# One input tile loaded in two column parts over two queues, and one late weight loaded whole

## The chip, the cores and the metric

The kernel runs on one core of one Trainium2 chip. The metric is device time in microseconds (us) of one execution. Inputs and outputs lie in HBM; all arrays are bfloat16.

## The reference

A block of a two-stream diffusion transformer: image tokens (2 x 256) and text tokens (2 x 32), width D = 1152. A condition vector `c` makes shift, scale and gate vectors for each stream.

```python
mod_i = (silu(c) @ wmod_img).reshape(B, 6, 1, D)
shi, sci, gai = mod_i[:, 0], mod_i[:, 1], mod_i[:, 2]
hi = layernorm(x_img) * (1 + sci) + shi
qi, ki, vi = split(hi @ wqkv_img, 3)
...
q = concat([qt, qi]); k = concat([kt, ki]); v = concat([vt, vi])
p = softmax(einsum('bqd,bkd->bqk', q, k) * D ** -0.5)
at, ai = split(einsum('bqk,bkd->bqd', p, v))
out_i = x_img + gai * (ai @ wo_img)
out_t = x_txt + gat * (at @ wo_txt)
```

The text stream is treated as the image stream, with its own weights. Only the first three of the six parts of `wmod_img` and `wmod_txt` are used.

## The kernel before

**Tiles.** The 512 image rows are four tiles of 128 rows (`x_i[:, i, :]`, i = 0 to 3, 288 KB each; tiles 0 and 1 are batch 0). D is cut into 9 blocks of 128 (`KT`) for contraction and into 3 chunks of 384 (`CH`) for statistics. Weights are [128, 9, 1152] tiles of 2592 KB; most of them rotate through a pool of five buffers (`wpool`, `load_w`, L73 to L77). Some 39 MB of weights go through in one execution.

**Order.** The schedule is written out by hand (`manual_schedule`, L62): each engine works through its instructions in program order, and a DMA is issued by the queue of the engine named in its call: `nc.sync` is SyncE (SP in the profile), `nc.scalar` is ScalarE (ACT). Waits between engines come from the tiles that the instructions read and write.

**The front, L80 to L116.** SyncE issues `c` (L81). Tiles 0 and 1 of x go on ScalarE's queue (L100). Then SyncE issues in this order: scale chunk 0 (`load_sc(0)`, blocks 0 and 1 of the image scale weight, 576 KB), x tile 2, two rows of the V weight (`load_v(0)`, 288 KB each), scale chunk 1, two V rows, scale chunk 2, two V rows, scale chunk 3 (864 KB), a V row, x tile 3, two V rows in one, and then the image shift weight and the image Q weight in three parts each. All later weights are issued by SyncE too (L433 to L443), each as soon as its buffer is free.

**The first work.** TensorE runs 15 warm-up matmuls on zeros (L286, L288) around the transpose of `c`. VectorE takes the layernorm statistics of tile 0, three instructions of 384 columns (`ln_stats`, L166), combines them (L171), does the same for tile 1, and then normalises tile 0 and tile 1 (L179). ScalarE takes the roots (L173). TensorE's program order is: the 18 matmuls of scale chunk 0 (`mod_scale(0)`, L218), the transposes of tile 0 (L197, L209), those of tile 1, and then V of the image tiles (`v_row`, L256; `v_narrow`, L268) between the matmuls of the further scale chunks. ScalarE scales the first two blocks while it moves them out of PSUM (`head_scaled`, L202).

**The V phase and after.** V is accumulated block by block as the V rows and scale chunks arrive, up to 28.5 us. The image shift follows (`mod_strip`, L404), then Q and K of the image (`qk_img`, L504), from 60 us on the text stream's shift and scale, then scores, softmax, attention output and the output projections.

**The text scale weight.** `w_sc_t` (L435) is loaded in two parts (`K2`: blocks 0 to 4, 1440 KB, and blocks 5 to 8, 1152 KB), after the text shift weight `w_sh_t` and ahead of the text tokens `x_t` (L436). It is read by the second `mod_strip` in `row_strips` (L522).

Of the kernel before, what the change touches and what calls it, by code (L numbers as in the profile page):

```python
# [14 lines left out]
def kernel(  # L15
# [14 lines left out]
    nc = tc.nc  # L30
# [4 lines left out]
    B, NI, D = x_img.shape  # L35
# [5 lines left out]
    TPB = NI // P  # L41
    NTT = B * NT
    CH = 384
# [24 lines left out]
    xi_t = xi_flat.rearrange("(i p) d -> p i d", p=P)  # L68

    def w_view(src):  # L70
        return src.rearrange("(kt p) n -> p kt n", p=P)

    def load_w(src, c0, ksplits=((0, KT),), home=None):  # L73
        t = wpool.tile([P, KT, D], bf, tag="w", name="t") if home is None else act.tile([P, KT, D], bf, tag=home, name="w_home")
        for (k0, k1) in ksplits:
            nc.sync.dma_start(t[:, k0:k1, :], w_view(src)[:, k0:k1, c0:c0 + D])
        return t  # L77
# [4 lines left out]
    x_i = act.tile([P, NIT, D], bf)  # L82
# [6 lines left out]
    def load_x(i, eng=nc.sync):  # L89
        eng.dma_start(x_i[:, i, :], xi_t[:, i, :])  # L90

    def load_sc(ch):
        k0, k1 = KC[ch]
        nc.sync.dma_start(w_sc_i[:, :, k0 * P:k1 * P], w_view(wmod_img)[:, :, D + k0 * P:D + k1 * P])
# [2 lines left out]
        for kt in range(*KC[ch]):  # L97
            nc.sync.dma_start(w_v_i[:, kt:kt + 1, :], w_view(wqkv_img)[:, kt:kt + 1, 2 * D:3 * D])

    for i in range(TPB):  # L100
        load_x(i, nc.scalar)
    load_sc(0)
    load_x(2)
    load_v(0)
# [9 lines left out]
    K2 = ((0, 5), (5, KT))  # L114
# [317 lines left out]

    w_k_i = load_w(wqkv_img, D, K3)  # L433
    w_sh_t = load_w(wmod_txt, 0)
    w_sc_t = load_w(wmod_txt, D, K2)  # L435
    nc.sync.dma_start(x_t[0:P:P // NTT, :], xt_flat[:, :])  # L436
    w_q_t = load_w(wqkv_txt, 0, K2)
    w_k_t = load_w(wqkv_txt, D, K2)
# [465 lines left out]
```

## Time and profile before

| | |
|---|---|
| three runs | 114.66, 114.88, 114.92 us; median 114.88 |
| the profiled execution | 114.55 us, span 112.7 us |
| TensorE matmul (PE) busy | 107.6 us, 95% of the span |
| TensorE weight load (PEld) busy | 64.1 us, 57% |
| VectorE (DVE) busy | 76.2 us, 68% |
| ScalarE (ACT) busy | 36.5 us, 32% |
| GpSimd (POOL) busy | 28.1 us, 25% |
| DMA | 40.87 MB, mean 363 GB/s over the span |
| SyncE's queue (q1) | 39.05 MB, 90.4% of the 16 DMA engines' span |
| granted TensorE clock | 1.0 throughout |

The span is the time from the first to the last instruction of the profiled execution; its own time is a little longer than that. PE and PEld are two rows for one engine, as weight loads overlap matmuls. A DMA of 128 rows is spread over 16 DMA engines, and it has landed when the last of them has reported. The chain of waits goes back from the last instruction to what released it, step by step.

### The profile page before, as it was taken

How to read it: one execution, taken by the hardware profiler on the slowest of the kernel's cores; microseconds unless marked ns; L12 is line 12 of the kernel's file. 1: busy time of each engine (PE TensorE's matmuls, PEld its weight loads, DVE VectorE, ACT ScalarE, POOL GpSimd, SP SyncE). 2: the span in 40 equal slices, each digit the busy share in tenths (PEclk: the TensorE clock that was granted, in tenths of full speed). 3: DMA queues.
4: the chain of work that ended last, by engine and by line, in shares of the span. 5: the costliest groups of instructions: out<-in, count | busy, mean ns of one | idle time of the engine just before them, and what ended most of it. 6: DMA issues, size and time to landing. Idle time of an engine off the chain costs nothing.

```text
span 112.7 us, 2837 instructions
## 1 busy us (share of the span) xinstructions
PE 107.6 (95%) x1182; PEld 64.1 (57%) x1191; DVE 76.2 (68%) x151; ACT 36.5 (32%) x83; POOL 28.1 (25%) x62
## 2 busy tenths in 40 slices
PE   5989999999999999999999999999999999999990
PEld 1356665565544444444446558787687565667670
DVE  1699330865499999999999950238657700899971
ACT  4527500471280080730009933024647700001000
POOL 7000120830230000000000161601540460499600
PEclk9999999999999999999999999999999999999999
DMA  3999999999999999999999999999999999994052
GB/s 90 321 376 347 373 373 407 409 413 411 405 410 408 411 410 413 404 412 410 413 410 414 413 403 408 404 398 404 410 407 401 411 422 394 383 371 168 7 192 70
DMA packets 22839, 40.87 MB, mean 363 GB/s; under 512 B 1375, under 2 KB 6635, under 8 KB 22827
## 3 DMA queue, kind: packets, MB, share of 16 engines
q1 hardware_dynamic: 21547, 39.05, 90.4%
q10 hardware_dynamic: 672, 0.77, 2.2%
q0 software_dynamic: 608, 0.88, 2.2%
q8 instruction: 9, 0.15, 0.5%
q14 instruction: 3, 0.02, 0.1%
HBM read 39.36 MB, written 1.34 MB: 361 GB/s over the span
## 4 chain that ended last, share of the span: by engine, by line
PE 89%; DVE 4%; DMA 3%; ACT 1%; issue 1%; ACTq 0%
PE qkps L504 31%; PE ps L826 16%; PE va L256 14%; PE aps L734 5%; PE ps L565 4%; PE sps L594 4%; PE gps L404 3%; DMA x_i<-in_x_img_dram 3%; DVE stats L166 3%; PE ops L844 2%; PE van L268 2%; PE ps L669 2%; PE mps L218 1%; ACT hT_i L202 1%; PE gps L799 1%; PE sps L607 1%
## 5 line engine op out<-in xcount | busy, mean ns | idle before, releaser
L504 PE MATMUL qkps<-hT_i,t 128*128 128x512 bf16 x158 | 35.4, 379 | 0.2
L504 PEld LDWEIGHTS <-t 128*128 128x128 bf16 x162 | 15.6, 98 | 18.7 <-DMA t<-in_wqkv_img_dram 0.3
L466 DVE SCALAR_TENSOR_TENSOR sacc<-w_v_i,mcols,sacc 128x1152 f32<-128x1152 bf16 x16 | 22.7, 1418 | 0.5
L256 PE MATMUL va<-w_v_i,hT_i 128*128 128x512 bf16 x67 | 17.0, 379 | 0.4 <-issue 0.2
L826 PE MATMUL ps<-t,aT 128*128 128x384 bf16 x99 | 16.4, 326 | 0.0
L826 PEld LDWEIGHTS <-aT 128*128 128x128 bf16 x117 | 11.0, 98 | 6.9 <-issue 0.5
L832 DVE TENSOR_TENSOR tmp<-ps,gb 128x384 bf16<-128x384 f32 x11 | 6.0, 548 | 6.5 <-DMA gb<-mod_scratch 6.0
L810 POOL TENSOR_TENSOR w_og<-t,gb 128x384 bf16<-128x384 bf16 x9 | 8.7, 1007 | 5.2 <-DMA gb<-mod_scratch 5.2
L256 PEld LDWEIGHTS <-hT_i 128*128 128x128 bf16 x72 | 6.4, 97 | 5.8 <-issue 0.2
L523 POOL TENSOR_SCALAR mod_txt<-mcols 128x18 f32<-128x18 f32 x2 | 0.6, 275 | 32.4 <-DVE mcols L410 32.4
L166 DVE BATCH_NORM_STATS2 stats<-x_i 128x6 f32<-128x384 bf16 x12 | 5.8, 541 | 2.6 <-DMA x_i<-in_x_img_dram 2.6
L454 ACT ACTIVATE qT<-qkps 128x512 bf16<-128x512 f32 x9 | 4.7, 601 | 6.9 <-PE qkps L504 6.9
L140 PE MATMUL wps<-wz 128*128 128x512 bf16 x15 | 5.6, 536 | 1.2 <-DVE wz L125 1.2
L470 ACT CAST shi<-sacc 128x1152 bf16<-128x1152 f32 x2 | 2.3, 1152 | 13.2 <-DVE sacc L466 13.2
L241 POOL TENSOR_SCALAR hT_i<-hT_i,mod_img 128x128 bf16<-128x128 bf16 (+1 forms) x5 | 2.1, 437 | 14.9 <-ACT hT_i L202 8.5
L747 DVE TENSOR_SCALAR aT<-aps,sv 128x288 bf16<-128x288 f32 (+2 forms) x11 | 4.3, 455 | 2.0 <-PE aps L734 2.0
L833 DVE TENSOR_TENSOR o<-tmp,x_i 128x384 bf16<-128x384 bf16 x11 | 5.3, 479 | 0.4
L565 PEld LDWEIGHTS <-t 128*128 128x128 bf16 x162 | 5.0, 98 | 0.5
L154 DVE CAST kT<-qkps 128x512 bf16<-128x512 f32 x3 | 2.1, 686 | 4.7 <-PE qkps L504 4.7
L565 PE MATMUL ps<-hT_t,t 128*128 128x64 bf16 x162 | 5.0, 193 | 0.0
L734 PE MATMUL aps<-pT,v_i 128*128 128x288 bf16 (+2 forms) x44 | 4.8, 264 | 0.0
L749 ACT ACTIVATE aT<-aps,sv 128x288 bf16<-128x288 f32 (+2 forms) x11 | 4.0, 468 | 2.1 <-PE aps L734 2.1
(150 smaller groups left out, 141.6 us busy)
## 6 DMA issues: line engine op xcount, KB each, us to landing
t<-in_wqkv_img_dram SPq DMA_DIRECT2D x6, 864.0 KB, 13.7
t<-in_wmod_txt_dram SPq DMA_DIRECT2D x2, 2592.0 KB, 18.2
t<-in_wqkv_txt_dram SPq DMA_DIRECT2D x2, 1440.0 KB, 14.3
t<-in_wmod_img_dram SPq DMA_DIRECT2D x3, 864.0 KB, 11.7
t<-in_wqkv_txt_dram SPq DMA_DIRECT2D x3, 864.0 KB, 14.0
t<-in_wo_txt_dram SPq DMA_DIRECT2D x3, 864.0 KB, 15.3
t<-in_wqkv_txt_dram SPq DMA_DIRECT2D x2, 1152.0 KB, 15.0
w_v_i<-in_wqkv_img_dram SPq DMA_DIRECT2D x7, 288.0 KB, 6.7
```

Source lines behind the costliest of these rows:

```text
L140: nc.tensor.matmul(ps[:], lhsT=wz[:, 0:P], rhs=wz[:], start=True, stop=True)
L166: nc.vector.bn_stats(stats[0:np_, k, :], x_ap[:, k * CH:(k + 1) * CH])
L256: nc.tensor.matmul(ps[:], lhsT=hT_i[:, kt, i * P:(i + 1) * P], rhs=w_v_i[:, kt, half * VW:(half + 1) * VW], start=(kt == 0), stop=(kt == K ...
L454: nc.scalar.mul(out_ap, in_ap, SCALE)
L466: nc.vector.scalar_tensor_tensor(saccs[b][:], w_v_i[:, kt, :], ap, saccs[b][:], op0=ALU.mult, op1=ALU.add)
L504: nc.tensor.matmul(pss[j - j0][:], lhsT=wq[:, kt, j * P:(j + 1) * P], rhs=hT_i[:, kt, :], start=(kt == 0), stop=(kt == KT - 1))
L565: nc.tensor.matmul(ps[:, j - j0, :], lhsT=wq[:, kt, j * P:(j + 1) * P], rhs=hT_t[:, kt, :], start=(kt == 0), stop=(kt == KT - 1))
L734: nc.tensor.matmul(bank[:, off:off + c1 - c0], lhsT=lhsT, rhs=rhs, start=(first[id(bank)] == n), stop=(final[id(bank)] == n))
L810: nc.gpsimd.tensor_mul(w_og[:, dt, 0:CH], w_o_i[:, dt, NG0:D], gb[:, B - 1, NG0:D])
L826: nc.tensor.matmul(ps[:, 0:cw], lhsT=aT[:, dt, t0:t0 + P], rhs=rhs, start=(dt == DTS[0]), stop=(dt == DTS[-1]))
L832: nc.vector.tensor_mul(tmp[:, 0:cw], ps[:, 0:cw], gb[:, b, cs])
L833: nc.vector.tensor_add(o[:, cs], tmp[:, 0:cw], x_i[:, i, cs])
```

## The change

Two places change. Tile 0 of x, one transfer of 128 x 1152 on ScalarE's queue, becomes two: columns 0 to 383 stay first on ScalarE's queue, and columns 384 to 1151 go on SyncE's queue, after `c` and ahead of scale chunk 0. Tile 1 stays on ScalarE's queue, behind the first part. The text scale weight `w_sc_t`, two transfers on SyncE's queue, becomes one of 2592 KB. The number of DMAs in the program stays the same. No arithmetic changes.

```diff
@@ -97,8 +97,9 @@
-    for i in range(TPB):
-        load_x(i, nc.scalar)
+    nc.scalar.dma_start(x_i[:, 0, 0:CH], xi_t[:, 0, 0:CH])
+    nc.sync.dma_start(x_i[:, 0, CH:D], xi_t[:, 0, CH:D])
+    load_x(1, nc.scalar)
     load_sc(0)
     load_x(2)
     load_v(0)
@@ -432,7 +433,7 @@
     w_k_i = load_w(wqkv_img, D, K3)
     w_sh_t = load_w(wmod_txt, 0)
-    w_sc_t = load_w(wmod_txt, D, K2)
+    w_sc_t = load_w(wmod_txt, D)
     nc.sync.dma_start(x_t[0:P:P // NTT, :], xt_flat[:, :])
```

## The prediction

> **What bounds the kernel now.** I read the times first: the profiled execution took 114.55 us with a span of 112.7, so 1.85 us lie around the span; the three runs have a median of 114.88, which is 0.33 above the profiled one. The sum below is made against 114.55 and then carried over as a difference. A measurement of this kernel can tell about 0.2% (0.23 us) from no change; the chances below use that bound.
>
> Second, the chain that ended last, in order of time (start, length, what). The reader sees that the first 8 us are one serial path: the first x tile lands, VectorE takes statistics of two tiles, normalises, TensorE transposes, ScalarE scales. After that the chain is TensorE alone.
>
> ```profile
> 0.73 3.00 DMA x_i<-in_x_img_dram
> ...
> 3.76 1.49 DVE stats L166 x3
> ...
> 5.51 1.34 DVE stats L166 x3
> ...
> 7.17 0.59 DVE xn_i L179
> ...
> 7.81 0.30 PE tph L197 x2
> ...
> 8.19 1.26 ACT hT_i L202 x4
> 9.46 1.44 PE va L256 x6
> ...
> 30.97 10.04 PE qkps L504 x46
> ```
>
> Third, SyncE's queue in order of time (start, length, instruction). Every weight goes through it, and until about 4 us it issues one transfer per 0.47 us; from 3.8 us on an issue itself takes up to 3 us, because the queue is full.
>
> ```profile
> 0.73 0.40 SPq L81 DMA_DIRECT2D c<-in_c_dram  x1
> 1.19 0.42 SPq L94 DMA_DIRECT2D w_sc_i<-in_wmod_img_dram  x1
> 1.66 0.68 SPq L90 DMA_DIRECT2D x_i<-in_x_img_dram  x1
> ...
> 3.82 2.16 SPq L98 DMA_DIRECT2D w_v_i<-in_wqkv_img_dram  x2
> ```
>
> Fourth, when TensorE first reads each weight, beside when it landed. These two timeline rows are the weight loads of the last scale chunk and of the image Q weight:
>
> ```profile
> 18.55 0.94 PEld L218 LDWEIGHTS <-w_sc_i 128*128 128x128 bf16 x27
> ...
> 30.76 5.22 PEld L504 LDWEIGHTS <-t 128*128 128x128 bf16 x25 [0.28 <-DMA t<-in_wqkv_img_dram]
> ```
>
> and these are the transfers (size, us from issue to landing), asked for in narrow windows around the issue times 1.14, 10.13 and 16.20:
>
> ```profile
> x_i<-in_x_img_dram ACTq DMA_DIRECT2D x1, 288.0 KB, 4.1
> w_sc_i<-in_wmod_img_dram SPq DMA_DIRECT2D x1, 864.0 KB, 8.4
> t<-in_wqkv_img_dram SPq DMA_DIRECT2D x1, 864.0 KB, 14.4
> ```
>
> So the last scale chunk landed at 10.13 + 8.4 = 18.5 and was read from 18.55; the first third of the Q weight landed at 16.20 + 14.4 = 30.6 and was read from 30.76, after a wait put down to that transfer. TensorE is 95% busy, and still it runs at most 0.1 to 0.2 us behind the weight stream at these two places. The same sum for the others: V rows of chunk 3 at 10.61 + 8.6 = 19.2, read from 19.42; scale chunk 2 at 13.8, read for 14.74. That is the fact I build on: the front of the kernel has two clocks, the x path and the weight stream, and they are almost level. The DMA rows of the page (9 in nearly every slice, about 410 GB/s) say that the stream can't go faster.
>
> **The change, part by part.** *First part of x tile 0 (384 of 1152 columns, 96 KB, ScalarE's queue).* Issued at 0.73 as before. A tile lands 3.0 us after issue. In the trace's packet records one row of 2304 B takes 93 ns and a 768 B piece (last scale chunk) 36 ns; each of 16 DMA engines has 8 rows, so this part needs 8 x 0.036 = 0.29 us in place of 0.74. It lands 0.45 sooner, at about 3.28, and the first of the three statistics (0.50 us each) runs from 3.3 to 3.8.
>
> *Second part (768 columns, 192 KB, SyncE's queue at 1.19).* The trace has no piece of 1536 B; between 36 and 93 ns a straight line gives 64 (estimate), so 0.51 us per engine. From below: if it behaves as tile 0 did, it lands 3.0 - 0.23 = 2.77 after issue, at 3.96; it could be at 3.7 if it finds the engines free. From above: the second tile, which shares the engines with a transfer of the other queue, needed 4.1, so 1.19 + 4.1 - 0.23 = 5.06. I take 3.96, nearer to tile 0's row, because now only 96 KB stand ahead of it. Statistics two and three then run from 4.0 to 5.0; before, the third ended at 5.25. Gain on VectorE 0.25; with the ends, +0.4 to -0.8. [...]
>
> *Tile 1* stays second on ScalarE's queue, issued at 1.14. It landed at 5.24 and its statistics started at 5.42. It is now wanted at 5.2. Its time is bounded by 3.0 (as tile 0, 4.1) and 4.1 (as before, 5.24). If it stays at 5.24 the gain on VectorE is 0.18 rather than 0.25. I keep 0.2.
>
> *What is moved back.* Scale chunk 0, tile 2, two V rows and scale chunk 1 are issued one SyncE step later, 0.47 each. Tile 2 lands 5.5 us after its issue against 3.0 for a transfer with nothing ahead, so there are 2.5 us of queue to hide 0.47; from 3.82 on SyncE is itself held up and the lateness is gone there. In bytes nothing changes: c, tile 0, tile 1 and scale chunk 0 are the same 1.13 MB ahead of everything else. What does change is 256 pieces for 128: 8 x (0.036 + 0.064 - 0.093) = 0.06 us per engine. Bounds for the shift of the whole stream: from below -0.1 (between 2.5 and 3.5 us the DMA share is 0.87 to 0.88, so about 0.12 us stood idle and may be filled); from above +0.4 (if an engine that is done with its short part finds nothing queued until SyncE's second part arrives: part one is over 0.45 sooner). I take +0.06. SyncE also waited 0.4 us, before scale chunk 2 at 6.40, for scale chunk 0 to land. With one transfer more at the front that wait may fall on a neighbour; behind it stand V rows that land 7 us later and are read later still, so it costs nothing while the queue is that deep.
>
> *Scale chunk 0* then lands at 1.19 + 5.2 + 0.06 = 6.45 rather than 6.39. The 18 small matmuls that read it ran from 6.69 to 7.28, and the transposes queued behind them on TensorE started at 7.81, when VectorE was done. Cover: 0.5 us before, 0.3 with VectorE 0.2 sooner. If it landed 0.3 or more later, that cover would be gone and the transposes would wait for TensorE.
>
> *Text scale weight whole.* It takes away one SyncE issue and one completion. The second half landed at 37.72 + 16.4 = 54.1; the 72 strip matmuls that read the two text weights run from 60.21 to 62.53, this weight in the second half of them. Some 7 us of cover; without it TensorE would wait up to 1152 KB at 410 GB/s, 2.8 us (estimate). The text tokens behind it (issued 42.56, 11.9 to landing, so 54.5) keep their place in the bytes. Cost nothing.
>
> *Sum.* The x path brings TensorE 0.2 us ahead at 9 us. The stream is 0.06 later. At the last scale chunk TensorE can come forward by what lies between landing and read, 18.55 - 18.5, and about 0.1 us of weight load done ahead: 0.1 to 0.15 in all; at the Q weight by 30.76 - 30.6 = 0.16, less the 0.08 that scale chunk 0 needed from landing (1.19 + 5.2 = 6.39) to its read (6.47), so 0.08. Less 0.06 of the stream, 0.0 to 0.1 of the 0.2 is left: I take 0.05. From 31 us on TensorE works without a DMA wait in the chain, so it arrives whole at the end: 114.55 - 0.05 = 114.50 beside the profiled execution, 114.83 beside the median.
>
> **The rivals.** *The whole gain comes through.* The waits at 18.55 and 30.76 may be mere starting time, as other changes of line cost 0.24 to 0.42 us of weight-load idle with no transfer named, and the stream may move up by its 0.1. Then the x path's gain decides, 0.2 to 0.5 if tile 1 also lands sooner (at 4.1 to 4.7, as nothing but tile 0's second part competes with it): 0.35, so 114.53. For it: tile 0 alone held VectorE until 3.76. Against it: the named wait at the Q weight.
>
> *The stream comes later (slower).* Place: the DMA engines between 2.3 and 3.5 us. If short first parts leave them empty before SyncE's second part arrives, or scale chunk 0's small pieces come after both tiles, every weight lands later by up to the 0.4 above, and TensorE waits for scale chunk 3, V rows of chunk 3 and the Q weight. It decides once the shift is over the 0.1 of room; beyond 0.33 it shows. With 0.4: +0.3, 115.18. For it: the second transfer on SyncE moved little before 2.7 us (DMA 203 GB/s from 2.0 to 2.5 us). Against it: tile 1 is queued on ScalarE and can fill the hole.
>
> *The change doesn't do what it says.* The second part lands at 4.3 or later, since tile 1's rows get ahead of it on the engines; then statistics two and three run at the old time and only the order of waiting has changed: 114.88, or 0.1 more.
>
> **How the numbers follow.** Forecast (capped by the stream) 0.33, whole gain 0.31, later stream 0.23, nothing done 0.13. Forecast and the last lie within 0.2%: 0.46; faster 0.31; slower 0.23. Time 114.83. The likeliest one's own range is 114.65 to 115.05 (a room of 0.0 to 0.15 and a stream shift of -0.1 to +0.2). As cases of both signs hold over half, the range reaches to 0.45 of gain and 0.35 of loss: 114.43 to 115.23.
>
> **What would show it.** The first statistic should start near 3.3 and the third end near 5.0, or it is the last rival. The load of the last scale chunk and that of the Q weight should start within 0.1 us of 18.5 and 30.7, with a DMA named ahead of them; a Q weight read well before 30.5 speaks for the whole gain, one after 31.0 for the late stream. Scale chunk 0 should land by 6.5. The text strips should start without a DMA wait; a wait there, or one anywhere behind 31 us, would make the prediction wrong in a way that I haven't priced.

## The result, and the profile after

The changed kernel takes 115.15 us (median of 22 runs) against 114.75 us for the kernel before (22 runs). The ratio is 1.0029, 95% interval 1.0019 to 1.0039: slower by 0.33 us by the ratio (the medians lie 0.40 apart), where 114.83 and no visible difference had been forecast. Timed again as a control beside other experiments, the same kernel came out at 1.0040 (1.0020 to 1.0059).

The profiled execution took 114.69 us (span 112.9). It is the fastest of the 22, so it shows the mechanism at its mildest, and further profiles of the same kernel are read below. First, VectorE's instructions in order of time (start, length, instruction; in brackets the idle time before it and what ended it):

```profile
2.85 0.56 DVE L167 BATCH_NORM_STATS2 stats<-x_i 128x6 f32<-128x384 bf16 x1 [1.69 <-DMA x_i<-in_x_img_dram]
3.90 1.02 DVE L167 BATCH_NORM_STATS2 stats<-x_i 128x6 f32<-128x384 bf16 x2 [0.50 <-DMA x_i<-in_x_img_dram]
...
6.86 0.58 DVE L180 TENSOR_SCALAR xn_i<-x_i,mv,rstd 128x1152 bf16<-128x1152 bf16 x1
```

The first statistic starts 0.9 us sooner than before (3.76), the other two wait half a microsecond for the second part, and the normalised tile is begun at 6.86 instead of 7.17. The x path has gained 0.31 us here. Now the chain that ended last, in order of time (start, length, what):

```profile
10.59 8.21 DMA w_sc_i<-in_wmod_img_dram
...
18.84 0.83 PE mps L219 x27
19.67 0.45 PE va L257 x2
...
31.05 29.24 PE qkps L505 x135
```

Before, the chain ran through the x tile, VectorE and ScalarE into TensorE. It now runs through SyncE's queue and the transfer of the last scale chunk (10.59 to 18.80), and the x path is not on it. The weight loads of that chunk and of the Q weight, from the timeline:

```profile
18.83 0.74 PEld L219 LDWEIGHTS <-w_sc_i 128*128 128x128 bf16 x27 [0.64 <-DMA w_sc_i<-in_wmod_img_dram]
...
30.84 1.12 PEld L505 LDWEIGHTS <-t 128*128 128x128 bf16 x6 [0.28 <-DMA t<-in_wqkv_img_dram]
```

The weight loads stand idle for 0.64 us until the chunk has landed and begin 0.28 later than before (18.55). A microsecond later, behind that chunk's matmuls, TensorE is 0.09 late (at 19.96 against 19.87), and Q then begins at 31.00, still 0.09 late (30.91). The 0.31 won at the front has turned into a wait, and a little more. The Q weight adds nothing to it, though a transfer is named at its loads: in another execution of the changed kernel (the first repetition below) that weight had landed at 16.90 + 13.8 = 30.7, and the same 0.28 us stand ahead of its loads with no transfer named:

```profile
31.32 0.25 PEld L505 LDWEIGHTS <-t 128*128 128x128 bf16 x2 [0.28 <-issue]
```

The stream itself is later; the same three stretches of both kernels show it (stretch; its length; per engine the busy time with the number of instructions; granted clock; DMA share; GB/s), before:

```profile
1.50:8.00 6.50, 5.97 (x38) 2.46 (x37) 4.10 (x12) 3.40 (x6) 1.50 (x6) 1.00 0.96 319
8.00:15.00 7.00, 6.85 (x71) 4.17 (x71) 4.40 (x14) 3.92 (x10) 0.48 (x1) 1.00 1.08 359
15.00:30.00 15.00, 14.71 (x167) 8.80 (x169) 6.91 (x18) 3.62 (x8) 3.93 (x13) 1.00 1.05 404
```

and after:

```profile
1.50:8.00 6.50, 5.91 (x43) 2.54 (x41) 4.51 (x12) 3.63 (x7) 1.50 (x6) 1.00 0.95 305
8.00:15.00 7.00, 6.85 (x77) 4.12 (x74) 4.09 (x14) 3.80 (x10) 0.48 (x1) 1.00 1.07 360
15.00:30.00 15.00, 14.86 (x163) 8.43 (x160) 6.83 (x18) 3.62 (x8) 3.93 (x13) 1.00 1.05 404
```

The last number of each row is what to read. From 8 us on the two move the same; up to 8 us the changed kernel moves 14 GB/s less, over 6.5 us some 91 KB, which at 404 GB/s is 0.23 us. In this execution that is not made up. Scale chunk 0 lands at 1.59 + 5.2 = 6.8 (before 1.19 + 5.2 = 6.4).

### The profile page after: what moved, and what is told of

It is laid out like the page before. It is cut to its first block, busy times and chain, and to the rows that moved or that the text cites. A ratio compares the mean times of both kernels' runs of the same rounds, so it can differ in the third digit from the quotient of the medians.

```text
span 112.9 us, 2845 instructions
## 1 busy us (share of the span) xinstructions
PE 108.0 (96%) x1191; PEld 63.9 (57%) x1191; DVE 75.9 (67%) x151; ACT 36.6 (32%) x83; POOL 28.1 (25%) x62
## 4 chain that ended last, share of the span: by engine, by line
PE 81%; SPq 8%; DMA 7%; issue 1%; DVE 0%
PE qkps L505 31%; PE ps L827 16%; PE va L257 7%; DMA w_sc_i<-in_wmod_img_dram 7%; SPq L98 6%; PE aps L735 5%; PE ps L566 4%; PE sps L595 4%; PE gps L405 3%; PE ops L845 2%; PE ps L670 2%; SPq L94 1%; PE van L269 1%; PE gps L800 1%; PE sps L608 1%; PE mps L219 1%
## 5 line engine op out<-in xcount | busy, mean ns | idle before, releaser
L505 PEld LDWEIGHTS <-t 128*128 128x128 bf16 x162 | 15.6, 98 | 18.7 <-DMA t<-in_wqkv_img_dram 0.3
L257 PE MATMUL va<-w_v_i,hT_i 128*128 128x512 bf16 x72 | 17.5, 379 | 0.0
L471 ACT CAST shi<-sacc 128x1152 bf16<-128x1152 f32 x2 | 2.3, 1152 | 13.2 <-DVE sacc L467 13.2
L141 PE MATMUL wps<-wz 128*128 128x512 bf16 x15 | 5.0, 492 | 1.2 <-DVE wz L126 1.2
L834 DVE TENSOR_TENSOR o<-tmp,x_i 128x384 bf16<-128x384 bf16 x11 | 4.7, 427 | 0.4
## 6 DMA issues: line engine op xcount, KB each, us to landing
t<-in_wqkv_txt_dram SPq DMA_DIRECT2D x2, 1440.0 KB, 14.2
```

Source lines behind the costliest of these rows:

```text
L141: nc.tensor.matmul(ps[:], lhsT=wz[:, 0:P], rhs=wz[:], start=True, stop=True)
L257: nc.tensor.matmul(ps[:], lhsT=hT_i[:, kt, i * P:(i + 1) * P], rhs=w_v_i[:, kt, half * VW:(half + 1) * VW], start=(kt == 0), stop=(kt == K ...
L505: nc.tensor.matmul(pss[j - j0][:], lhsT=wq[:, kt, j * P:(j + 1) * P], rhs=hT_i[:, kt, :], start=(kt == 0), stop=(kt == KT - 1))
```

## The experiments

Two theories stood at the start. Theory S: the weight stream comes later because of what is done at the front, and TensorE waits for weights. Rival W: the text scale weight loaded whole is what costs; rival L: the number of transfers is; rival X: the x path still sets the end. After the first four runs rival Q joined them: tile 0's second part often lands late, so that the x path has no gain. Each ratio is to the kernel before on the same chip.

**Which half of the change.** The x part alone (the edit below, made in the changed kernel), and the text scale weight alone (the reverse edit, made in the kernel before):

```diff
-    w_sc_t = load_w(wmod_txt, D)
+    w_sc_t = load_w(wmod_txt, D, K2)
```

> Only the x part of the change: tile 0 in two parts on two queues, the text scale weight still in two transfers. Theory S (the weight stream comes later because of the split at the front): as the whole change, 0.2 to 0.4 us slower than before, scale chunk 3 landing near 18.8 instead of 18.5. Rival W (the text scale weight loaded whole is what costs): within 0.1 us of before. Rival L (the number of transfers, odd against the rotation of completion semaphores, is what costs): slower than the whole change.

> Only the other part: the kernel before with the text scale weight in one transfer. Theory S: within 0.1 us of before, front landings unchanged (scale chunk 3 at 18.5). Rival W: 0.2 to 0.4 us slower.

The split alone takes 116.09 us, ratio 1.0107 (1.0086 to 1.0127), far more than the whole change. The whole weight alone takes 114.94, ratio 1.0012 (0.9998 to 1.0025), no difference beyond its interval, though by that interval alone W could still have a quarter of a per cent. What speaks against W is the profile of the x part alone, which shows the loss at the front without the whole weight. VectorE, and the waits of the weight loads (line waited at, for what: us in all, times, longest):

```profile
6.78 0.58 DVE L180 TENSOR_SCALAR xn_i<-x_i,mv,rstd 128x1152 bf16<-128x1152 bf16 x1
...
PEld L219 <- DMA w_sc_i<-in_wmod_img_dram: 1.1, 2, 0.7
...
PEld L505 <- DMA t<-in_wqkv_img_dram: 0.5, 1, 0.5
```

The x path is 0.39 us ahead of before there, the loads wait for two scale chunks and for the Q weight, and Q begins at 31.30, 0.39 late. L holds in part: with the whole weight the split costs about 0.3 us, and without it, with one transfer more in the program, some 0.9 us on top. These are at the end of the program. SyncE's own waits show one piece of it. The x part alone:

```profile
SPq L900 <- PEq L900: 0.7, 2, 0.5
```

and before:

```profile
SPq L899 <- SPq L899: 0.5, 1, 0.5
...
SPq L899 <- PEq L899: 0.2, 1, 0.2
```

From the end of the last VectorE addition to the end of the span the x part alone needs 114.35 - 110.95 = 3.40 us, the kernel before 112.74 - 110.28 = 2.46 and the whole change 112.91 - 110.45 = 2.46. Two things make up the 0.94. In the trace's records SyncE ends by waiting for the eight rotating completion semaphores in a fixed order, some 0.06 us each. With the count as before the last store is on the last of them; with one transfer more it is on the first, and the others are gone through after it has landed (112.44 to 112.93). The other half lies between the closing instructions that follow: the kernel before has one pause of about half a microsecond there (its first row, put down to SyncE itself), the x part alone has two (113.02 to 113.47, and the 0.5 in its row). In the fourteen profiles of this case this closing part goes with the number of transfers that SyncE issues: 0.91 to 0.92 us with 50 of them (seven profiles, before and changed among them), 1.07 to 1.08 with 49 (five), 1.39 to 1.40 with 51 (two, the x part alone being one). Why it does so wasn't tried.

**Does the x path matter at all?** The whole change with the gain on VectorE taken back by one more statistic:

```diff
-    stats_of(0, 0, NCH)
+    stats_of(0, 0, NCH - 1)
+    nc.vector.bn_stats(lns[0][0:P, NCH - 1, :], x_i[:, 0, D - CH:D - CH + 208])
+    stats_of(0, NCH - 1, NCH)
```

> The whole change, with one more VectorE statistic of 208 columns (about 0.3 us) ahead of the third one of tile 0, which takes back about what VectorE had gained. Theory S: TensorE waits for weights anyway, so the time stays within 0.1 us of the whole change, and the wait for scale chunk 3 shrinks from 0.64 us by about 0.3. Rival X (the x path still sets the end): 0.3 us more than the whole change.

It takes 115.27 us, ratio 1.0033 (1.0015 to 1.0050), about as the whole change does; if the x path set the end, 0.3 us more would make it 1.0055 (1.0029 + 0.0026), which the interval leaves out, but not by much. The changed kernel wasn't timed beside it, so the timed runs speak for S without proving it. The profile of this run (115.58 us, above the median of its runs) shows another case: tile 0's second part landed only at 1.20 + 3.6 = 4.8, the chain went through VectorE, and Q began 1.03 later than before. The wait for the last scale chunk did shrink, to 0.21 us, but because TensorE came to it late. That brought up rival Q.

**Is it SyncE's queue?** Both parts on ScalarE's queue:

```diff
-    nc.sync.dma_start(x_i[:, 0, CH:D], xi_t[:, 0, CH:D])
+    nc.scalar.dma_start(x_i[:, 0, CH:D], xi_t[:, 0, CH:D])
```

> The whole change, but both parts of tile 0 on ScalarE's queue, the first ahead of the second, tile 1 behind them; SyncE issues scale chunk 0 as early as before. Theory S in the form that SyncE's queue order is the cause: the stream is back where it was, landing of scale chunk 0 near 6.4 and of chunk 3 near 18.5, time within 0.15 us of before or a little faster. Rival P (the smaller pieces or a third transfer at the front are the cause, on any queue): 0.2 to 0.4 us slower as the whole change.

Neither came true for the time: 115.88 us, ratio 1.0111 (1.0068 to 1.0153), slower than both theories allowed, for a reason that the transfers of its profile (of an execution of 116.64 us) show (KB, us from issue to landing):

```profile
x_i<-in_x_img_dram ACTq DMA_DIRECT2D x1, 192.0 KB, 5.0
x_i<-in_x_img_dram ACTq DMA_DIRECT2D x1, 96.0 KB, 2.2
```

The first part landed 2.2 us after issue, the second 5.0, at 6.1 us. In the trace's packet records the 512 B pieces of scale chunk 0, on SyncE's queue, begin at 2.30 and those of the second part only at 3.65; from 3.75 to 5 us 577 of the former end beside 83 of the latter. VectorE began the second statistic at 6.15. A second transfer on the quiet queue was not next in line. It also says why the change puts the second part on SyncE ahead of scale chunk 0. The stream, however, did what S expected: scale chunks 0, 1 and 2 landed at 6.3, 10.7 and 13.9 us (before 6.4, 10.6 and 13.8; changed 6.8, 11.1 and 14.2), and what the front moved less up to 8 us (299 GB/s) was largely made up from 8 to 15 (373 against 359).

**The spread of the changed kernel.** The same kernel profiled again, twice, and once more as the control of the last set:

> The changed kernel again, for a second profile: its profiled execution of 114.69 us was the fastest of its 22 runs (median 115.15). Theory S: an execution of 115.1 or more shows the last scale chunk landing later than 18.8 and TensorE waiting for it. Rival Q (tile 0's second part on SyncE's queue often lands late and then the x path itself is later than before): such an execution shows the second part landing after 4.3 us, not near 3.9, and tile 0's third statistic ending after 5.25.

> The same once more, for the spread: Theory S wants the second part below 4.3 us and the stream late; rival Q the second part above 4.3 us in the slower executions.

> The changed kernel itself, timed on the same chip as the three others: 0.2 to 0.4 us above before by both theories.

| profiled execution | time, us | tile 0 complete | GB/s, 1.5 to 8 us | first Q matmul |
|---|---|---|---|---|
| before | 114.55 | 3.7 | 319 | 30.91 |
| before, text weight whole | 114.94 | 3.8 | 317 | 30.97 |
| changed | 114.69 | 3.9 | 305 | 31.00 |
| changed, again 1 | 115.07 | 4.8 | 303 | 31.47 |
| changed, again 2 | 114.97 | 4.2 | 299 | 31.37 |
| changed, control | 114.96 | 4.2 | 288 | 31.35 |
| changed, tile 1 behind (below) | 115.74 | 3.6 | 287 | 31.52 |
| changed, one statistic more (above) | 115.58 | 4.8 | 311 | 31.94 |
| x part alone (above) | 116.13 | 3.8 | 306 | 31.30 |

Both columns in the middle are worse in all four executions of the changed kernel, and the last column follows the time: once Q has begun, 83.6 to 83.7 us remain in the kernel before and in the changed one. The landing of the last scale chunk says the same as the GB/s: 18.5 and 18.7 us in the first two rows, 18.8, 19.3, 19.2 and 18.9 in the four of the changed kernel. In the first repetition the second part came late enough for the x path to hold TensorE, as rival Q has it. VectorE in it:

```profile
2.74 0.56 DVE L167 BATCH_NORM_STATS2 stats<-x_i 128x6 f32<-128x384 bf16 x1 [1.58 <-DMA x_i<-in_x_img_dram]
4.78 1.02 DVE L167 BATCH_NORM_STATS2 stats<-x_i 128x6 f32<-128x384 bf16 x2 [1.47 <-DMA x_i<-in_x_img_dram]
...
7.73 0.58 DVE L180 TENSOR_SCALAR xn_i<-x_i,mv,rstd 128x1152 bf16<-128x1152 bf16 x1
```

The first statistic is as early as ever; the other two wait 1.47 us, and the normalised tile is begun 0.56 later than before; TensorE is 0.56 late from its first transposes on and still so at Q. In the other two the x path is level with before (7.20 and 7.21 against 7.17). In the second repetition the weight loads wait 0.74 us for the last scale chunk, and TensorE is 0.03 late ahead of it and 0.45 behind it. In the control they wait 0.62 for scale chunk 1, and 0.04 becomes 0.44:

```profile
11.83 0.52 PEld L219 LDWEIGHTS <-w_sc_i 128*128 128x128 bf16 x18 [0.62 <-DMA w_sc_i<-in_wmod_img_dram]
```

So three of the four executions of the changed kernel are held by the stream, as S has it, and one by the late second part.

**The stream relieved.** Both kernels without the load of x tile 2 (tile 1 stands in for it), which takes 288 KB off the front of the stream (the lines that put tile 1 in its place are left out here):

```diff
-    load_x(2)
...
```

> The kernel before without the load of x tile 2 (288 KB, 0.7 us of the stream); tile 1 is used in its place, so the result of tile 2 is left out. All weights behind it land 0.7 us sooner. If the front before is held by the x path as much as by the stream (as the sum had it), the gain is small: 0 to 0.2 us below before.

> The changed kernel without the load of x tile 2, tile 1 in its place. Theory S: the stream no longer holds TensorE, so what the x path gains shows: 0.2 to 0.3 us below the kernel before without tile 2. Rival Q: the x path has no gain in most executions, so it is no faster than the kernel before without tile 2, or slower.

The kernel before falls to 114.78, ratio 0.9990 (0.9979 to 1.0000); the changed one to 114.91, ratio 1.0001 (0.9983 to 1.0019). In neither profile does TensorE wait for a scale chunk. The loss is about 0.1% instead of 0.29%, with intervals that overlap, so that it shrank is likely and not shown; on this chip the changed kernel itself ran only twice, at 115.07 and 114.97 against 114.92. No gain appeared, which is against S's figure and for Q: in this profile the second part landed at 1.20 + 3.0 = 4.2, where the third statistic ends when it used to. The two profiles can't be set beside each other, as they are of a fast execution of the changed kernel (114.72) and of the slowest of the other (114.96).

**The stream burdened, with the x path untouched.** The kernel before with 96 KB more:

```diff
     load_x(2)
+    nc.sync.dma_start(xf_full[:, 0:CH], xi_t[:, 3, 0:CH])
```

> The kernel before with 96 KB more in SyncE's queue, behind x tile 2 (a copy that nobody reads before it is written over), and the text scale weight whole so that the number of transfers stays even with before. The x path is untouched; the stream behind tile 2 is 8 pieces of 0.036 us per engine, 0.29 us, later: about what the changed kernel's stream has lost (some 85 KB, 0.2 us). Theory S (a later stream is enough to explain the loss): 0.15 to 0.3 us above before. Rival Q (the late second part of tile 0 explains it, and the stream has room): within 0.1 us of before.

It takes 115.03 us, ratio 1.0021 (1.0006 to 1.0037): 0.24 us for 0.29 us of stream, as S expects; the whole text weight, which is in this kernel too, may have 0.1% of it. That the loss came through the stream isn't shown. In the only profile, of the slowest of its 12 runs (115.75 us), tile 1 landed late, VectorE waited 1.05 us for it, and TensorE was 1.20 late from its first transposes on without a wait for a weight behind them: there the extra bytes did touch the x path.

**The second part made early.** In one kernel it is issued first on SyncE and the condition vector moved to ScalarE's queue; in the other tile 1 is moved behind it:

```diff
-    load_x(1, nc.scalar)
+    load_x(1)
```

> The changed kernel with tile 0's second part first on SyncE's queue, and the condition vector moved to ScalarE's queue between the first part and tile 1. The second part is issued at 0.73 instead of 1.19. Rival Q: it lands by 3.7 in every execution, the x path gains 0.3, and the time falls to before or below it. Theory S: scale chunk 0 is back at its old issue time, so the stream is about 0.1 late at most; TensorE still waits for weights, and the time comes within 0.15 us of before, not below it by more than 0.1.

> The changed kernel with tile 1 on SyncE's queue behind tile 0's second part, ahead of scale chunk 0, so that nothing of ScalarE's queue competes with the second part. Rival Q: the second part lands by 3.7 and the time falls to before or below. Theory S: the stream is as late as in the changed kernel (scale chunk 0 behind both), so the time stays 0.2 to 0.4 us above before.

The first takes 116.24 us, ratio 1.0126 (1.0097 to 1.0155), against both expectations. Its profile is of its slowest execution (118.69 us) and can only hint: tile 1, now third on ScalarE's queue, landed 6.0 us after issue, at 7.8. The second takes 116.25, ratio 1.0132 (1.0097 to 1.0167), far more than either expected; its profile, of the fastest of its six runs (115.74), decides between Q and S for the front. The second part landed at 3.6, tile 1 at 4.6, and VectorE began to normalise at 6.59, earlier than in any other run here:

```profile
6.59 0.58 DVE L180 TENSOR_SCALAR xn_i<-x_i,mv,rstd 128x1152 bf16<-128x1152 bf16 x1
```

Yet Q began at 31.52, 0.61 later than before. The weight loads that TensorE waited for:

```profile
19.36 0.74 PEld L219 LDWEIGHTS <-w_sc_i 128*128 128x128 bf16 x27 [0.62 <-DMA w_sc_i<-in_wmod_img_dram]
...
31.38 0.10 PEld L505 LDWEIGHTS <-t 128*128 128x128 bf16 x1 [0.30 <-DMA t<-in_wqkv_img_dram]
```

An x path 0.6 us ahead was worth nothing here, as the stream was late: 287 GB/s up to 8 us against 318 make 0.5 us by the same working as above. TensorE loses time at scale chunk 0 (landed at 2.08 + 5.1 = 7.2), at chunk 1 and at the last one. The rest of this execution's loss is the second closing pause seen in the x part alone, as here too SyncE issues 51 transfers: 113.96 - 111.03 = 2.93 against 2.46. The half microsecond between this execution and the median of its runs isn't in any profile. No kernel here that does the whole work beats the one before: the front has two clocks that are level, and the edits that brought the x path forward made the stream later.

## Why the prediction was wrong

The picture of two level clocks was right, and the last scale chunk is where TensorE waited. Two terms of the sum were mis-sized, and together they turn the sign; a third step was read wrongly and didn't matter.

**The shift of the stream**, the step "I take +0.06". Only the piece overhead was priced. The front moved 305, 303, 299 and 288 GB/s in four profiles against 319 and 317: a mean of 19 less over 6.5 us, 125 KB, 0.31 us at 404 GB/s. Some 25 KB of it come back from 8 to 15 us (360, 356, 364 and 362 against 359 and 355), which leaves 0.25. The upper bound of +0.4 covered it, and the rival "the stream comes later" had its time (115.18) and its first wait, the last scale chunk, right; it was given 0.23. Its place, a hole ahead of 3.5 us, is only part of it, as the last paragraph of this section shows.

**The gain of the x path**, 0.2 us. The mechanism was right and in the profiled execution the gain was even larger: the first statistic at 2.85 (forecast 3.3), the second part at 3.9 (3.96), the third statistic's end at 4.92 (5.0), TensorE's first V matmuls 0.31 sooner. But the second part landed at 3.9, 4.8, 4.2 and 4.2, a mean of 4.3, and at 4.2 there is nothing left of the gain. The bound from tile 1's row (5.06) was closed to 0.3 us in one execution of four, and the value taken (3.96) was about the best of the four rather than their middle. The 3.7 given there for free engines was no floor: with tile 1 behind it on SyncE's queue, tile 0 was complete at 3.6.

**The wait at the Q weight.** It was taken as the second place where the stream holds TensorE. In none of the four executions of the changed kernel does TensorE lose time there: it is as late at the first Q matmul as behind the last scale chunk, to 0.01 us: 0.09, 0.56, 0.46 and 0.44. The 0.28 us of idle weight loads that the prediction read as a wait also stand there with no transfer named. Only in the x part alone, where the weight landed at 17.86 + 13.4 = 31.3, did it cost something (0.33 late before it, 0.39 at Q).

**What held.** From 31 us on the difference arrived whole at the end. The range (114.43 to 115.23) holds 115.15 only by its upper end, which was set for the later stream. The cover of scale chunk 0 was just enough in the profiled execution, though mis-sized too: the chunk landed at 6.8, 0.4 later instead of 0.06, and its 18 matmuls ended at 7.40, just ahead of the transposes at 7.50. The text scale weight whole cost nothing that could be measured. What the step on it missed is the other side: the text priced only a wait of TensorE, while without this half the change would have been slower by 0.9 us more at the end of the program.

**The rivals.** The whole gain never came through: at the last scale chunk the wait was real. At the Q weight its guess of mere starting time was right. "The change doesn't do what it says" is the first repetition, with the second part at 4.8; it was priced at 0.1, and it was worth 0.5 there.

What stays open: why the stream loses those 125 KB. Piece overhead is 0.06 us of the 0.31: in the packet records of the changed kernel the median piece of 768, 1536 and 2304 B takes 36, 65 and 93 ns, and 8 x (0.036 + 0.065 - 0.093) is 0.06. The DMA share up to 8 us hardly differs (0.95, 0.97, 0.94 and 0.93 in the changed kernel, 0.96 and 0.98 in the two others), so the engines are about as long at work and move less. When it happens varies: the profiled execution moved 277 GB/s from 1.5 to 5 us (before 275) and 338 from 5 to 8 (before 371), the first repetition 261 and 352. In the trace's packet records the slowest single read of 2304 B between 5 and 8 us takes 0.71 to 1.18 us in the four changed profiles, where most take 0.093; in the kernel before the slowest takes 0.33, with the text weight whole 0.72. The second part's place in SyncE's queue has to do with it, as with both parts on ScalarE's the stream was on time up to scale chunk 2, but there the tile also came 2 us later. Why these reads are slow wasn't tried, nor how much of the loss in the mean is due to the late second part.

## What to carry to other kernels

Here a transfer moved ahead of a queue of weights that keeps TensorE just fed was paid by what stood behind it: the last scale chunk landed at 18.8 to 19.3 us in the changed kernel and at 18.5 before. In such a place compare each landing with its first use, and price the moved bytes and the gaps against the smallest of those margins. The tile split over two queues was complete only when its later part had landed, 2.7 to 3.6 us after issue in the four executions with tile 1 on the other queue and 2.4 in the one with tile 1 behind it, so take the spread of the neighbouring rows and not the best of them. The closing part took 0.91 to 0.92 us with 50 transfers issued by SyncE, 1.07 to 1.08 with 49 and 1.39 to 1.40 with 51: after a change to the number of transfers in a program, or to the queue of one, look at its last microseconds too.

## What the runs showed of the hardware

With both parts of the tile on one queue the DMA engines did not take one piece from each queue in turn: the second part landed 5.0 us after its issue and the first 2.2, and from 3.75 to 5 us, while both queues moved, 577 pieces of 512 B of the other queue ended beside 83 of the second part. In what order an engine serves the queues wasn't measured beyond that.

An issue on SyncE took longer with more of its pieces under way, which is what the prediction calls a full queue: in the records of the kernel before, the issue of a V row of 288 KB took 0.43 to 0.44 us with 1280 to 1791 pieces issued and not yet ended, and 1.69 to 2.79 us with 2393 to 2769.

The end of the program came out longer with one transfer more: 3.40 us from the last addition to the end of the span, against 2.46 with the count as before. About half of the 0.94 is the place of the last store's completion semaphore in the order in which SyncE waits for them (0.49 us, 112.44 to 112.93), and half a second closing pause (0.45, 113.02 to 113.47), whose cause is open. And the landing of one and the same transfer varied: tile 0's second part, 192 KB with the same issue time, landed 2.7 to 3.6 us after issue in four executions of one kernel.
